# Seven products for five of the eight chunk pairs of a cosine layer, with the features kept in float32 until the last layer

## The chip, the cores and the metric

One core of one Trainium2 chip runs the program. The metric is the device time of one execution in microseconds (us), before and after the change.

## The reference

Causal attention (2 batches of 448 tokens, 12 heads of 64) is followed by a gated layer and by a layer with a cosine. What the change touches is the end:

```python
    gate = 1.0 / (1.0 + np.exp(-(x @ w_gate)))   # x: 896 x 768, w_gate and w_val: 768 x 1536
    val = x @ w_val
    x = gate * val @ w_out                        # w_out: 1536 x 768
    h = x @ w_in                                  # w_in: 768 x 2048
    g = h * np.cos(h)
    return g @ w_out2                             # 2048 x 768
```

(`w_in` and `w_out2` are the arrays `moe2_w_in` and `moe2_w_out`.) Inputs and output are of double and single precision; products must come out with nearly float32 accuracy.

## The kernel before, in words

Features lie on partitions, the 448 tokens of one batch on the free dimension. TensorE multiplies 128x128 blocks of weights (stationary) by 128x448 blocks of features (moving). To get nearly float32 accuracy, every float32 operand is split into a high and a low part: ScalarE rounds (`hi`), VectorE subtracts (`lo = x - hi`), and one product is three matmuls, hi·hi, hi·lo and lo·hi (`products`, lines 223 to 230). So one output block of 128 features for one batch in a layer with 768 inputs is 6 x 3 = 18 matmuls, a *group*.

The weights come from HBM in *chunks* (one block of outputs, up to six blocks of inputs) as raw 64-bit words. Each chunk is loaded by SyncE (line 144, two buffers `wraw`), decoded into float32 by ScalarE (upper half `up`, line 165) and VectorE (`wf`, line 167), and split into `whi` (ScalarE, line 176) and `wlo` (VectorE, line 178); four buffers each. `advance` (line 219) splits one chunk, decodes the next and loads the one after.

The order of the work is written out by hand. Each engine runs its own queue strictly in the order in which the program issues to it, and waits on semaphores. The stages:

- Attention, 0 to about 75 us.
- The gate layer (lines 544 to 647). Its first two of twelve outputs are plain, the other ten are *units* of class `Unit`: Strassen's algorithm on 2x2 blocks, where the two outputs are the gate and the value block, the two halves of the inputs are even and odd chunks (order `KORD`), and the two columns are the two batches. Seven products of 3 x 3 = 9 matmuls (`product`, line 491) replace eight. The price is sums of weights (`sums12`, `sums34`, 384 wide), three split weights per unit instead of two, and sums that are carried through PSUM banks: `after(n)` copies or adds a bank once product n is there, for instance line 537 adds bank `b` and the copy `s5` into a new bank `c`, and product 7 then goes on in bank `b`, product 3 in `c`. The products of a unit are issued in the order 1, 5, 2, 6, 4, 7, 3, where product 4 is the previous unit's; the first unit has no previous one and runs 1, 5, 6, 2, 7, 3. Between two products `emit` issues what follows the product before.
- The output layer (lines 655 to 670): 432 matmuls, two output blocks at a time, each split into `X2` at once.
- The cosine layer (lines 701 to 711): 16 outputs, two batches, plain groups. `post` follows each group on ScalarE and VectorE: `turns` (line 678 rounds h/2pi to an integer, line 679 subtracts it), `cosine` one group later (Sin at line 683, multiply by the bank at 684), and `split` of the feature g two groups later (lines 233 and 234).
- The last layer (lines 713 to 732): six outputs, one after the other, each over three chunks and two batches, then a copy and the output DMA.

Of the kernel before, what the change touches and what calls it, by code (L numbers as in the profile page):

```python
# [2 lines left out]

# [17 lines left out]
P = 128  # L21
# [14 lines left out]
KP = KX // 2  # L36
WH = KP * P
PLAIN = 2

FIRST_ROWS = {2: (0, 3), 4: (3, 5)}  # L40
FIRST_ROWS_END = 5
# [29 lines left out]
def attn_moe_moe2(  # L71
# [337 lines left out]
    early = ExitStack()  # L409
    epool = early.enter_context(tc.tile_pool(name="epool", bufs=1))  # L410
    epool.tile([P, 48], F32, tag="pad", name="pad")

    def temp(tag, bufs):
# [42 lines left out]
    class Unit:  # L456

        def __init__(self, f):
            self.f = f

        def parts(self, src):
            hi, lo = weights("whi"), weights("wlo")
# [35 lines left out]
                mm(ps[:, :S], lhsT=lo[:, blk], rhs=r[:, 0], start=False, stop=stop, skip_group_check=True)  # L498

        def p(self, n):  # L500
            x = [[XB[b][2 * j + o] for j in range(KP)] for o, b in ((0, 0), (1, 0), (1, 1))]
            if n == 1:
                self.a = bank()
                self.product(self.a, self.A, 0, x[0], True, True)
            elif n == 2:
                self.product(self.a, self.A, 1, x[1], False, True)
            elif n == 3:
                self.product(self.c, self.S34, 1, x[2], False, True)
            elif n == 4:
                self.product(self.e, self.A22, 0, T[3], False, True)  # L510
            elif n == 5:
                self.d = bank()
                self.product(self.d, self.S12, 0, T[0], True, True)
            elif n == 6:
                self.product(self.b, self.S12, 1, T[1], False, True)
            else:
                self.product(self.b, self.S34, 0, T[2], False, True)

        def after(self, n):
            if n == 1:  # L520
                self.b = bank()
                nc.scalar.copy(self.b[:, :S], self.a[:, :S])
            elif n == 2:
                self.sg0 = temp("sg", 4)
                nc.scalar.activation(self.sg0, self.a[:, :S], AF.Sigmoid)
            elif n == 3:
                sg1 = temp("sg", 4)
                nc.scalar.activation(sg1, self.c[:, :S], AF.Sigmoid)
                gated(self.f, 1, sg1, self.tmp)
            elif n == 4:  # L530
                gated(self.f, 0, self.sg0, self.e[:, :S])
            elif n == 5:
                self.s5 = temp("s5", 2)
                nc.scalar.copy(self.s5, self.d[:, :S])
            elif n == 6:
                self.c = bank()
                nc.vector.tensor_tensor(self.c[:, :S], self.b[:, :S], self.s5, op=ALU.add)
            else:
                self.e = bank()
                nc.scalar.copy(self.e[:, :S], self.b[:, :S])  # L540
                self.tmp = temp("tmp", 2)
                nc.vector.tensor_tensor(self.tmp, self.e[:, :S], self.s5, op=ALU.add)

    for f in range(PLAIN):
        sg = []
        if f:
            wt = next_chunk()
            pg = []
            advance()
        else:  # L550
            decode_load()
        for b in range(B):
            if f:
                pg.append(bank())
                products(pg[b], wt, xr[b], True, True)
            sg.append(temp("sg", 4))
            nc.scalar.activation(sg[b], pg[b][:, :S], AF.Sigmoid)
            run(3)
        wt = next_chunk()
        if f == PLAIN - 1:  # L560
            words = [singles[2 * PLAIN].w]
        advance()
        if f == PLAIN - 1:
            unit = Unit(PLAIN)
# [37 lines left out]
    def emit(u, n):  # L602
        u.p(n)
        if done:
            v, m = done.pop()
            v.after(m)
        done.append((u, n))

    old = None
    unit.A = next_chunk()  # L610
    for f in range(PLAIN, KH):
        new, last = Unit(f + 1), f == KH - 1
# [30 lines left out]
        unit, old = new, unit  # L643
    emit(old, 4)
    split_h(1)
    old.after(4)
    early.close()

    gpool = ctx.enter_context(tc.tile_pool(name="gpool", bufs=1))
    tpool = ctx.enter_context(tc.tile_pool(name="tpool", bufs=2))  # L650

    at_chunk["split"] = at_chunk["use"] = 2 * KH
    parts[step("split")] = new.A
    singles[2 * KH + 1] = k1
    X2 = [[None] * KX for b in range(B)]
    nch = KH // WC
    for m in range(0, KX, 2):
        ps2 = [[bank() for i in range(2)] for b in range(B)]
        for c in range(nch):
            wts = [next_chunk()]  # L660
            for b in range(B):
                advance()
                for i in range(2):
                    if i and not b:
                        wts.append(next_chunk())
                    products(ps2[b][i], wts[i], H[b][c * WC : c * WC + WC], c == 0, c == nch - 1)
                    split_h(3)
                    if c == nch - 1:
                        X2[b][m + i] = slot(f"f{2 * (m + i) + b}", f"y{m + i}{b}")
                        split(X2[b][m + i], ps2[b][i][:, :S])  # L670

    quarter = tpool.tile([P, 1], F32, tag="quarter", name="quarter", bufs=1)
    nc.vector.memset(quarter, TWOPI / 4)

    def turns(ph):
        r = tpool.tile([P, S], F32, tag="t1", name="r", bufs=3)
        n = r.bitcast(I32)
        nc.scalar.activation(n, ph[:, :S], AF.Copy, scale=INV2PI, bias=0.25)  # L678
        nc.vector.scalar_tensor_tensor(r, ph[:, :S], INV2PI, n, op0=ALU.mult, op1=ALU.subtract)  # L679
        return r  # L680

    def cosine(ph, r):
        nc.scalar.activation(r, r, AF.Sin, scale=TWOPI, bias=quarter)
        nc.vector.tensor_tensor(r, r, ph[:, :S], op=ALU.mult)

    GTAG = [f"g{i}" for i in range(8)] + list(HTAGS)
    G = [[None] * KG for b in range(B)]
    units = {}
    nu = KG * B

    def post(u):
        if u < nu:
            units[u].append(turns(units[u][0]))
        if 0 <= u - 1 < nu:
            cosine(*units[u - 1])
        if 0 <= u - 2 < nu:
            f, b = divmod(u - 2, B)
            G[b][f] = slot(GTAG.pop(0), f"g{f}{b}")
            split(G[b][f], units.pop(u - 2)[1])

    for f in range(KG):
        wt = next_chunk()
        for b in range(B):
            u = f * B + b
            units[u] = [bank()]
            products(units[u][0], wt, X2[b], True, True)
            if b == 0:
                advance()
            post(u)
    post(nu)  # L710
    post(nu + 1)

    nch = (KG + WC - 1) // WC
    for m in range(KX):
        ps2 = [bank(), bank()]
        for c in range(nch):
            wt = next_chunk()
            advance()
            for b in range(B):
                products(ps2[b], wt, G[b][c * WC : min(KG, c * WC + WC)], c == 0, c == nch - 1)  # L720
                if c == nch - 1:
                    o = tpool.tile([P, S], F32, tag="t0", name="o")
                    rows, c0 = slice(m * P, m * P + P), b * S
                    if m == KX - 1 and b == B - 1:

                        nc.scalar.copy(o[:, : S // 2], ps2[b][:, : S // 2])
                        nc.vector.tensor_copy(o[:, S // 2 :], ps2[b][:, S // 2 : S])
                        nc.scalar.dma_start(out=out[rows, c0 : c0 + S // 2], in_=o[:, : S // 2])
                        nc.sync.dma_start(out=out[rows, c0 + S // 2 : c0 + S], in_=o[:, S // 2 :])
                    else:  # L730
                        nc.scalar.copy(o, ps2[b][:, :S])
                        nc.sync.dma_start(out=out[rows, c0 : c0 + S], in_=o)

def _layouts(inputs):
# [19 lines left out]
    def blocks(w):  # L756
# [32 lines left out]
```

## Time and profile before

| | |
|---|---|
| median of 3 runs | 553.76 us (553.63 to 553.77) |
| profiled execution | 553.79 us, its span 551.9 us |
| TensorE busy (PE) | 545.4 us, 99%, 3104 matmuls |
| VectorE busy (DVE) | 334.0 us, 61% |
| ScalarE busy (ACT) | 301.7 us, 55% |
| GpSimd busy (POOL) | 59.2 us, 11% |
| DMA | 68.14 MB, mean 123 GB/s |

Busy time counts the time in which an engine works on an instruction. The span goes from the first to the last instruction that the profiler recorded; the execution's time holds some 1.9 us more around it. PEld is TensorE's weight load, which overlaps its matmuls. All times of rows count from the span's start.

### The profile page before, as it was taken

How to read it: one execution, taken by the hardware profiler on the slowest of the kernel's cores; microseconds unless marked ns; L12 is line 12 of the kernel's file. 1: busy time of each engine (PE TensorE's matmuls, PEld its weight loads, DVE VectorE, ACT ScalarE, POOL GpSimd, SP SyncE). 2: the span in 40 equal slices, each digit the busy share in tenths (PEclk: the TensorE clock that was granted, in tenths of full speed). 3: DMA queues.
4: the chain of work that ended last, by engine and by line, in shares of the span. 5: the costliest groups of instructions: out<-in, count | busy, mean ns of one | idle time of the engine just before them, and what ended most of it. 6: DMA issues, size and time to landing. Idle time of an engine off the chain costs nothing.

```text
span 551.9 us, 8126 instructions
## 1 busy us (share of the span) xinstructions
PE 545.4 (99%) x3104; PEld 489.1 (89%) x3104; DVE 334.0 (61%) x624; ACT 301.7 (55%) x579; POOL 59.2 (11%) x131
## 2 busy tenths in 40 slices
PE   8999999999999999999999999999999999999997
PEld 5666679989999999999999999999999999999996
DVE  4889959987777777873324257777777722312310
ACT  5898955675555665853323267666666632422320
POOL 4788850000000000000000000000000000000000
PEclk9999999999999999999999999999999999999999
DMA  8745114264433333351515123333333234532500
GB/s 337 261 147 211 50 58 130 99 184 142 132 115 115 114 116 115 115 172 57 173 57 172 47 69 116 113 115 114 116 114 97 83 113 143 186 116 87 169 34 33
DMA packets 14725, 68.14 MB, mean 123 GB/s; under 512 B 1632, under 2 KB 3808, under 8 KB 14688
## 3 DMA queue, kind: packets, MB, share of 16 engines
q1 hardware_dynamic: 14400, 67.33, 37.1%
q8 instruction: 24, 0.39, 0.3%
q10 hardware_dynamic: 288, 0.31, 0.2%
q14 instruction: 13, 0.11, 0.1%
HBM read 64.88 MB, written 2.75 MB: 123 GB/s over the span
## 4 chain that ended last, share of the span: by engine, by line
PE 97%; POOL 1%; ACT 1%; DVE 1%; issue 0%; ACTq 0%; POOLq 0%
PE ps L230 21%; PE ps L229 21%; PE ps L228 21%; PE ps L496 8%; PE ps L497 8%; PE ps L498 8%; PE ps L326 4%; PE ps L342 4%; PE ps L302 3%; POOL pbuf L286 1%; ACT pbuf L310 1%; PE ps L256 1%; DVE ps L306 0%; DVE rs L283 0%; POOL sums L282 0%
## 5 line engine op out<-in xcount | busy, mean ns | idle before, releaser
L178 DVE TENSOR_TENSOR wlo<-wf,whi 128x768 fp32r<-128x768 f32 (+2 forms) x51 | 47.3, 927 | 61.6 <-ACT whi L176 60.1
L165 ACT ACTIVATE up<-wraw 128x768 f16<-128x768 bf16 (+2 forms) x71 | 74.2, 1046 | 12.1 <-DMA wraw<-in_w_out_dram 10.7
L167 DVE SCALAR_TENSOR_TENSOR wf<-wraw,up 128x768 uint32<-128x768 uint32 (+2 forms) x71 | 66.9, 942 | 22.4 <-ACT up L165 21.8
L230 PE MATMUL ps<-g,wlo 128*128 128x448 f32 x192 | 69.7, 363 | 0.0
L230 PE MATMUL ps<-y,wlo 128*128 128x448 f32 x192 | 69.7, 363 | 0.0
L229 PE MATMUL ps<-y,whi 128*128 128x448 f32 x192 | 69.6, 362 | 0.0
L229 PE MATMUL ps<-g,whi 128*128 128x448 f32 x192 | 69.6, 362 | 0.0
L228 PE MATMUL ps<-y,whi 128*128 128x448 f32 x192 | 69.1, 360 | 0.0
L228 PE MATMUL ps<-g,whi 128*128 128x448 f32 x192 | 69.1, 360 | 0.0
L230 PE MATMUL ps<-h,wlo 128*128 128x448 f32 x144 | 52.3, 363 | 0.0
L229 PE MATMUL ps<-h,whi 128*128 128x448 f32 x144 | 52.2, 362 | 0.0
L228 PE MATMUL ps<-h,whi 128*128 128x448 f32 x144 | 51.8, 360 | 0.0
L176 ACT ACTIVATE whi<-wf 128x768 fp32r<-128x768 f32 (+2 forms) x51 | 41.0, 804 | 14.9 <-DVE wf L167 14.9
L310 ACT ACTIVATE pbuf<-ps,nm 128x64 f32<-128x64 f32 (+6 forms) x84 | 38.6, 482 | 9.6 <-DVE nm L306 9.1
L286 POOL TENSOR_SCALAR pbuf<-pbuf,rs 128x64 f32<-128x64 f32 (+6 forms) x84 | 39.1, 488 | 9.4 <-PE ps L302 6.3
L679 DVE SCALAR_TENSOR_TENSOR r<-ps,r 128x448 f32<-128x448 f32 x32 | 19.9, 621 | 31.3 <-ACT r L678 31.3
L678 ACT ACTIVATE r<-ps 128x448 int32<-128x448 f32 x32 | 17.4, 545 | 38.9 <-PE ps L230 38.9
L229 PEld LDWEIGHTS ps<-y,whi 128*128 128x128 f32 x192 | 36.0, 188 | 2.9
L229 PEld LDWEIGHTS ps<-g,whi 128*128 128x128 f32 x192 | 36.0, 188 | 2.9
L228 PEld LDWEIGHTS ps<-g,whi 128*128 128x128 f32 x192 | 35.9, 187 | 2.6
L228 PEld LDWEIGHTS ps<-y,whi 128*128 128x128 f32 x192 | 35.9, 187 | 2.4
L230 PEld LDWEIGHTS ps<-y,wlo 128*128 128x128 f32 x192 | 36.0, 188 | 2.0
(96 smaller groups left out, 1089.4 us busy)
## 6 DMA issues: line engine op xcount, KB each, us to landing
wraw<-in_w_gv_dram SPq DMA_DIRECT2D x24, 768.0 KB, 4.3
wraw<-in_w_out_dram SPq DMA_DIRECT2D x24, 768.0 KB, 4.4
wraw<-in_w_in_dram SPq DMA_DIRECT2D x16, 768.0 KB, 4.3
qkv<-in_qkv_dram SPq DMA_DIRECT2D x9, 928.0 KB, 5.9
wraw<-in_w_out_dram SPq DMA_DIRECT2D x6, 512.0 KB, 3.9
out_dram<-o SPq DMA_DIRECT2D x11, 224.0 KB, 2.0
qkv<-in_qkv_dram SPq DMA_DIRECT2D x3, 256.0 KB, 6.8
qkv<-in_qkv_dram SPq DMA_DIRECT2D x1, 672.0 KB, 6.4
```

The costliest lines, as they stand in the source:

```text
L165: nc.scalar.activation(up.bitcast(F16)[:, 1::2], self.top[:, e0:e1], AF.Copy)
L167: nc.vector.scalar_tensor_tensor(self.w[:, e0:e1].bitcast(U32), self.mid[:, e0:e1], 13, up.bitcast(U32), op0=ALU.logical_shift_right, op1= ...
L176: nc.scalar.activation(self.hi[:, e0:e1], self.w[:, e0:e1], AF.Copy)
L178: nc.vector.tensor_tensor(self.lo[:, e0:e1], self.w[:, e0:e1], self.hi.bitcast(F32)[:, e0:e1], op=ALU.subtract)
L228: mm(ps[:, :S], lhsT=hi[:, blk], rhs=r[:, 0], start=first and k == 0, stop=False)
L229: mm(ps[:, :S], lhsT=hi[:, blk], rhs=r[:, 1], start=False, stop=False)
L230: mm(ps[:, :S], lhsT=lo[:, blk], rhs=r[:, 0], start=False, stop=last and k == n - 1)
L286: nc.gpsimd.tensor_scalar(row, row, rs[:, i : i + 1], 1.0, op0=ALU.mult, op1=ALU.mult)
L310: nc.scalar.activation(pb[:, POFF[i] : POFF[i] + w], ps[:, :w], AF.Exp, scale=-1.0, bias=nm[:, i : i + 1], accum_out=sums[:, i : i + 1],)
L496: mm(ps[:, :S], lhsT=hi[:, blk], rhs=r[:, 0], start=start, stop=False, skip_group_check=True)
L497: mm(ps[:, :S], lhsT=hi[:, blk], rhs=r[:, 1], start=False, stop=False, skip_group_check=True)
L498: mm(ps[:, :S], lhsT=lo[:, blk], rhs=r[:, 0], start=False, stop=stop, skip_group_check=True)
```

## The change

`Unit` becomes a general class `Product` (features X and their sums T are its arguments), and the gate layer's units a subclass `Gate` that does the same as before. A second subclass `Pair` takes two output chunks of the cosine layer together. The string `KINDS` says for each of the eight pairs whether it goes by seven products (S: pairs 1, 2, 4, 5, 6, counted from 0) or plainly (P: pairs 0, 3, 7). The output layer makes also the sums of its results that the products need (`U2`, split into `T2`). The features g are no longer split when they are made but kept in float32 (`GF`), and split later (`split_g`): seven in the last pair, the rest in the last layer. That layer takes two outputs at a time, so each pair of chunks is used by four groups before the next. `w_in` comes in the order `KORD`.

```diff
+KINDS = "PSSPSSSP"
...
-    for m in range(KX):
+    for m in range(0, KX, 2):
         for c in range(0, KG, WC):
             n = min(WC, KG - c)
-            chunks.append((w_out2[m, :, c : c + n], n))
+            for i in range(2):
+                chunks.append((w_out2[m + i, :, c : c + n], n))
...
+    def block_of_x(j, ps, b, i):
+        X2[b][2 * j + i] = slot(XTAG[j][2 * b + i], f"y{2 * j + i}{b}")
+        split(X2[b][2 * j + i], ps[b][i][:, :S])
+        if not i:
+            if not b:
+                U2[j] = [slot(tag, "u", F32) for tag in UTAG[j]]
+            nc.scalar.copy(U2[j][0][:, b], ps[b][i][:, :S])
+            if b:
+                u1 = U2[j][0][:, 0]
+                difference(u1, ps[1][0][:, :S], u1)
+
+    def sums_of_block(j, ps):
+        (u1, u3), (u2, u4) = [[t[:, i] for i in range(2)] for t in U2[j]]
+        for dst, a, b in ((u3, ps[1][1], u3), (u2, ps[1][1], u1), (u4, ps[0][1], u2)):
+            difference(dst, a[:, :S], b)
+            yield
+
+    def parts_of_block(j):
+        (u1, u3), (u2, u4) = [[t[:, i] for i in range(2)] for t in U2[j]]
+        for i, u in enumerate((u1, u2, u3, u4)):
+            T2[i][j] = slot(TTAG[j][i], f"T{i}{j}")
+            split(T2[i][j], u)
+            yield
...
+    def cosines():
+        if turned:
+            h, r, (f, b) = turned.pop(0)
+            if GF[f] is None:
+                GF[f] = slot(GFTAG.pop(0), f"g{f}", F32)
+            nc.scalar.activation(r, r, AF.Sin, scale=TWOPI, bias=quarter)
+            nc.vector.tensor_tensor(GF[f][:, b], r, h, op=ALU.mult)
+        if due:
+            h, fb = due.pop(0)
+            r = temp("sg", 4)
+            n = r.bitcast(I32)
+            nc.scalar.activation(n, h, AF.Copy, scale=INV2PI, bias=0.25)
+            nc.vector.scalar_tensor_tensor(r, h, INV2PI, n, op0=ALU.mult, op1=ALU.subtract)
+            turned.append((h, r, fb))
...
+        def result(self, n):
+            f = self.f
+            if n == 2:
+                due.append((self.a[:, :S], (f, 0)))
+            elif n == 3:
+                due.extend([(self.c[:, :S], (f, 1)), (self.tmp, (f + 1, 1))])
+            elif n == 4:
+                due.append((self.e[:, :S], (f + 1, 0)))
...
+        if seven:
+            order = (1, 5, 2, 6, 4, 7, 3) if old else (1, 5, 6, 2, 7, 3)
+        else:
+            order = (8, 9, 4) + tuple(range(10, 16)) if old else tuple(range(8, 16))
+        for at, n in enumerate(order):
+            emit(old if n == 4 else unit, n)
+            cosines()
+            if at == 0:
+                if seven:
+                    unit.high22()
+                    k0 = upper_of()
+                    unit.sums34()
...
+            elif at == 1:
+                if seven:
+                    unit.S34 = unit.parts(unit.s34)
+                    unit.low22()
...
+                w0 = word_of(k0)
+            elif at == 2:
+                k1 = upper_of()
+                if seven:
+                    unit.low(unit.S34, unit.s34)
+            elif at == 3:
+                new.A = unit.parts(w0)
+                new.w = w0, word_of(k1)
+            elif at == 4 and new_seven:
+                new.sums12()
+            elif at == 5:
+                if new_seven:
+                    new.S12 = new.parts(new.s12)
+                unit.low(new.A, w0)
+            if at == min(len(order) - 1, 6) and new_seven:
+                new.low(new.S12, new.s12)
+            run(1)
+            if last and at > 1:
+                split_g(1)
...
+                for i in range(2):
+                    if i and not b:
+                        wts.append(next_chunk())
+                    g, m = G[b][c * WC : min(KG, c * WC + WC)], 2 * j + i
+                    products(ps2[b][i], wts[i], g, c == 0, c == nch - 1)
+                    cosines()
+                    split_g(3)
...
-        "w_in2": blocks(inputs["moe2_w_in"]),
+        "w_in2": blocks(inputs["moe2_w_in"])[:, :, list(KORD)],
```

Products 8 to 15 are the halves (9 matmuls) of a plain pair's four groups. After the change line 429 is `difference`, 171 and 182 are the decode and the low part in `Chunk`, 478 the first sum of `sums12`, 533 the sum for bank `c`, 538 that for `tmp`, 743 the subtraction of turns and 737 the multiply by the Sin.

First place: VectorE's queue in a plain pair of chunks of the cosine layer before. `wf` is a decoded chunk, `r` the turns and then the cosine, `g` a feature's split.

```order
L178 TENSOR_TENSOR wlo<-wf_3313,whi 128x768
L167 SCALAR_TENSOR_TENSOR wf_3375<-wraw,up 128x768
L679 SCALAR_TENSOR_TENSOR r<-ps,r 128x448
L684 TENSOR_TENSOR r<-r,ps 128x448
L234 TENSOR_TENSOR g_3384<-r,g_3384 128x448
```

And the second half of pair 4 in the changed kernel, which has six products (in the order 1, 5, 6, 2, 7, 3) because a plain pair stands before it:

```order
L533 TENSOR_TENSOR ps<-ps,s_3823 128x448
L171 SCALAR_TENSOR_TENSOR wf_3825<-wraw,up 128x768
L743 SCALAR_TENSOR_TENSOR sg<-ps,sg 128x448
L478 TENSOR_TENSOR s_3856<-wf_3825 128x384
L429 TENSOR_TENSOR s_3856<-s_3856,wf_3789 128x384
L538 TENSOR_TENSOR tmp<-ps,s_3823 128x448
L737 TENSOR_TENSOR g_3872<-sg,ps 128x448
L429 TENSOR_TENSOR wlo<-wf_3789,whi 128x768
L429 TENSOR_TENSOR wlo<-s_3856,whi 128x768
```

The split of the feature has gone, sums of weights and a second low part have come in, and a cosine's multiply (line 737) stands between the sum for `tmp` and the low part of the next pair's first weights.

Second place: VectorE's queue in pair 5 from the first subtraction of turns to the sum for bank `c` (line 533), on whose bank product 7 goes on.

```order
L743 SCALAR_TENSOR_TENSOR sg<-ps,sg 128x448
L429 TENSOR_TENSOR s_3897<-wf_3789,wf_3825 128x384
L429 TENSOR_TENSOR s_3897<-wf_3789,s_3856 128x384
L737 TENSOR_TENSOR g_3872<-sg,ps 128x448
L743 SCALAR_TENSOR_TENSOR sg<-tmp,sg 128x448
L429 TENSOR_TENSOR a_3893<-wf_3825,a_3893 128x384
L171 SCALAR_TENSOR_TENSOR wf_3895<-wraw,up 128x768
L737 TENSOR_TENSOR g_3934<-sg,tmp 128x448
L429 TENSOR_TENSOR wlo<-s_3897,whi 128x768
L743 SCALAR_TENSOR_TENSOR sg<-ps,sg 128x448
L171 SCALAR_TENSOR_TENSOR wf_3937<-wraw,up 128x768
L533 TENSOR_TENSOR ps<-ps,s_3932 128x448
```

In the gate layer the same stretch has one operation of 448 (the gated product) ahead of the two sums and none of the four others of lines 737 and 743 behind them.

## Rows read from the trace of the kernel before

**Rows 1.** The page: busy time of the engines, and the chain that ended last, by engine.

```profile
PE 545.4 (99%) x3104; PEld 489.1 (89%) x3104; DVE 334.0 (61%) x624; ACT 301.7 (55%) x579; POOL 59.2 (11%) x131
...
PE 97%; POOL 1%; ACT 1%; DVE 1%; issue 0%; ACTq 0%; POOLq 0%
```

**Rows 2.** Timeline of TensorE where the cosine layer begins: start, duration (us), line, operation.

```profile
317.60 0.36 PE L230 MATMUL ps<-h,wlo 128*128 128x448 f32 x1
317.80 0.36 PE L228 MATMUL ps<-y,whi 128*128 128x448 f32 x1
```

**Rows 3.** Windows (us; PE, PEld, DVE, ACT, POOL busy): output, cosine, last layer, gate unit.

```profile
231.30:317.80 86.50, 86.50 (x434) 81.08 (x433) 38.25 (x52) 33.38 (x50) 0.00 (x0) 1.00 0.35 110
317.80:433.00 115.20, 115.20 (x577) 107.98 (x576) 81.41 (x124) 76.28 (x124) 0.00 (x0) 1.00 0.32 105
433.00:548.20 115.20, 115.20 (x577) 107.79 (x575) 31.30 (x39) 36.13 (x50) 0.00 (x0) 1.00 0.34 110
...
153.80:166.40 12.60, 12.60 (x64) 11.81 (x63) 9.36 (x15) 7.30 (x11) 0.00 (x0) 1.00 0.39 125
```

**Rows 4.** Timeline of VectorE in a unit of the gate layer.

```profile
155.12 0.55 DVE L425 TENSOR_TENSOR s<-wf,wf 128x384 f32<-128x384 f32 x1
155.59 0.55 DVE L425 TENSOR_TENSOR s<-wf,s 128x384 f32<-128x384 f32 x1
...
156.53 0.95 DVE L167 SCALAR_TENSOR_TENSOR wf<-wraw,up 128x768 uint32<-128x768 uint32 x1
157.40 0.95 DVE L425 TENSOR_TENSOR wlo<-s,whi 128x768 fp32r<-128x768 f32 x1
...
161.74 0.55 DVE L474 TENSOR_TENSOR s<-wf 128x384 f32<-128x384 f32 x1
162.32 0.56 DVE L425 TENSOR_TENSOR s<-s,wf 128x384 f32<-128x384 f32 x1
```

**Rows 5.** Timeline of ScalarE and VectorE behind a group of the cosine layer.

```profile
350.40 0.55 ACT L678 ACTIVATE r<-ps 128x448 int32<-128x448 f32 x1 [0.32 <-PE ps L230]
...
350.84 0.66 ACT L683 ACTIVATE r<-r,quarter 128x448 f32<-128x448 f32 x1
...
350.99 0.62 DVE L679 SCALAR_TENSOR_TENSOR r<-ps,r 128x448 f32<-128x448 f32 x1
...
351.54 0.62 DVE L684 TENSOR_TENSOR r<-r,ps 128x448 f32<-128x448 f32 x1
```

**Rows 6.** Timeline of ScalarE in the unit of rows 4.

```profile
154.44 0.52 ACT L485 ACTIVATE a<-wf 128x384 fp32r<-128x384 f32 x1
154.86 1.08 ACT L165 ACTIVATE up<-wraw 128x768 f16<-128x768 bf16 x1
155.80 0.57 ACT L522 COPY ps<-ps 128x448 f32<-128x448 f32 x1
156.30 0.85 ACT L463 ACTIVATE whi<-s 128x768 fp32r<-128x768 f32 x1
```

**Rows 7.** Timelines of VectorE and TensorE at the end of the gate layer's first unit.

```profile
111.40 0.63 DVE L537 TENSOR_TENSOR ps<-ps,s 128x448 f32<-128x448 f32 x1
...
114.74 0.62 DVE L542 TENSOR_TENSOR tmp<-ps,s 128x448 f32<-128x448 f32 x1 [0.68 <-ACT ps L540]
115.29 0.95 DVE L425 TENSOR_TENSOR wlo<-wf,whi 128x768 fp32r<-128x768 f32 x1
...
112.08 0.47 PE L496 MATMUL ps<-T,whi 128*128 128x448 f32 x1
112.39 0.37 PE L497 MATMUL ps<-T,whi 128*128 128x448 f32 x1
...
116.29 0.47 PE L498 MATMUL ps<-x,wlo 128*128 128x448 f32 x1
116.60 0.36 PE L496 MATMUL ps<-x,whi 128*128 128x448 f32 x1
```

**Rows 8.** Groups of VectorE in the cosine layer: busy us, mean ns, idle before, releaser.

```profile
L679 DVE SCALAR_TENSOR_TENSOR r<-ps,r 128x448 f32<-128x448 f32 x31 | 19.3, 621 | 29.4 <-ACT r L678 29.4
```

More of the change, by code (lines that the diff above doesn't have):

```diff
@@ L509, in p, with behind @@
             elif n == 4:
-                self.product(self.e, self.A22, 0, T[3], False, True)
+                self.product(self.e, self.A22, 0, self.T[3], False, True)
             elif n == 5:
                 self.d = bank()
-                self.product(self.d, self.S12, 0, T[0], True, True)
+                self.product(self.d, self.S12, 0, self.T[0], True, True)
             elif n == 6:
-                self.product(self.b, self.S12, 1, T[1], False, True)
+                self.product(self.b, self.S12, 1, self.T[1], False, True)
             else:
-                self.product(self.b, self.S34, 0, T[2], False, True)
-        def after(self, n):
+                self.product(self.b, self.S34, 0, self.T[2], False, True)
+        def behind(self, n):
             if n == 1:
@@ L522, in after, with __init__ @@
                 nc.scalar.copy(self.b[:, :S], self.a[:, :S])
-            elif n == 2:
+            elif n == 5:
+                self.s5 = temp("s5", 2)
+                nc.scalar.copy(self.s5, self.d[:, :S])
+            elif n == 6:
+                self.c = bank()
+                nc.vector.tensor_tensor(self.c[:, :S], self.b[:, :S], self.s5, op=ALU.add)
+            elif n == 7:
+                self.e = bank()
+                nc.scalar.copy(self.e[:, :S], self.b[:, :S])
+                self.tmp = temp("tmp", 2)
+                nc.vector.tensor_tensor(self.tmp, self.e[:, :S], self.s5, op=ALU.add)
+            else:
+                self.result(n)
+    class Gate(Product):
+        def __init__(self, f):
+            Product.__init__(self, XB, T)
+            self.f = f
+        def result(self, n):
+            if n == 2:
                 self.sg0 = temp("sg", 4)
@@ L529, in after @@
                 gated(self.f, 1, sg1, self.tmp)
-            elif n == 4:
+            else:
                 gated(self.f, 0, self.sg0, self.e[:, :S])
[L532 to L542, printed above, removed]
     for f in range(PLAIN):
@@ L605, in emit @@
             v, m = done.pop()
-            v.after(m)
+            v.behind(m)
         done.append((u, n))
@@ L611, in attn_moe_moe2 @@
     for f in range(PLAIN, KH):
-        new, last = Unit(f + 1), f == KH - 1
+        new, last = Gate(f + 1), f == KH - 1
         order = (1, 5, 2, 6, 4, 7, 3) if old else (1, 5, 6, 2, 7, 3)
@@ L645, in attn_moe_moe2 @@
     split_h(1)
[L646 to L650, printed above, removed]
+    old.behind(4)
+    done.pop()
     at_chunk["split"] = at_chunk["use"] = 2 * KH
@@ L682, in cosine @@
[L682 to L686, printed above, removed]
-    G = [[None] * KG for b in range(B)]
[L688 to L707, printed above, removed]
-                advance()
[L709 to L732, printed above, removed]
@@ new lines, in attn_moe_moe2, with split_g @@
+    GTAG = ["b4", "f7", "b0", "b5", "f8", "b1", "t3", "f9", "b2", "t4", "t13", "t14"] + sum(XTAG, [])
+    GORD = [(k, b) for c in range(0, KG, WC) for b in range(B) for k in range(c, min(KG, c + WC))]
+    GFREE = ["t5", "t6", "t7", "t8", "b6", "b7", "b8", "t9", "t10", "t11", "g2", "g3", "f4", "f5"]
+    G = [[None] * KG for b in range(B)]
+    def split_g(n):
+        for i in range(n):
+            if GORD:
+                k, b = GORD.pop(0)
+                G[b][k] = slot(GTAG.pop(0), f"g{k}{b}")
+                split(G[b][k], GF[k][:, b])
+                if b == B - 1 and GFREE:
+                    GTAG.append(GFREE.pop(0))
@@ new lines, in attn_moe_moe2, with __init__, p, result @@
+    class Pair(Product):
+        def __init__(self, u):
+            Product.__init__(self, X2, T2)
+            self.f = 2 * u
+            self.xr = [[X2[b][k] for k in KORD] for b in range(B)]
+            self.banks = {}
+        def p(self, n):
+            if n <= 7:
+                return Product.p(self, n)
+            i, b, half = (n - 8) // 4, (n - 8) // 2 % 2, n % 2 == 1
+            if not half:
+                self.banks[i, b] = bank()
+            ks = range(half * KP, half * KP + KP)
+            products(self.banks[i, b], self.C if i else self.A, self.xr[b], not half, half, ks)
+        def result(self, n):
+            f = self.f
+            if n == 2:
+                due.append((self.a[:, :S], (f, 0)))
[3 more added lines that the diff above has]
+                due.append((self.e[:, :S], (f + 1, 0)))
+            elif n % 2:
+                i, b = (n - 8) // 4, (n - 8) // 2 % 2
+                due.append((self.banks[i, b][:, :S], (f + i, b)))
@@ new lines, in attn_moe_moe2 @@
+    c3 = at_chunk["use"]
+    unit, old = Pair(0), None
+    unit.A = next_chunk()
+    unit.w = None, singles.pop(c3 + 1).w
+    for u, kind in enumerate(KINDS):
+        new, last = Pair(u + 1), u == len(KINDS) - 1
+        seven = kind == "S"
+        new_seven = not last and KINDS[u + 1] == "S"
+        if seven:
+            order = (1, 5, 2, 6, 4, 7, 3) if old else (1, 5, 6, 2, 7, 3)
+        else:
+            order = (8, 9, 4) + tuple(range(10, 16)) if old else tuple(range(8, 16))
[7 more added lines that the diff above has]
+                    unit.sums34()
+                else:
+                    unit.C = unit.parts(unit.w[1])
+                    k0 = upper_of()
+            elif at == 1:
+                if seven:
+                    unit.S34 = unit.parts(unit.s34)
+                    unit.low22()
+                else:
+                    unit.low(unit.C, unit.w[1])
+                w0 = word_of(k0)
[14 more added lines that the diff above has]
+                new.low(new.S12, new.s12)
+            run(1)
+            if last and at > 1:
+                split_g(1)
+        unit, old = new, unit if seven else None
@@ new lines, in attn_moe_moe2 @@
+    c4 = c3 + KG
+    at_chunk["split"] = at_chunk["use"] = c4
+    parts[step("split")] = unit.A
+    singles[c4 + 1] = k1
+    v, n = done.pop()
+    v.behind(n)
+    nch = (KG + WC - 1) // WC
+    for j in range(KP):
+        ps2 = [[bank() for i in range(2)] for b in range(B)]
+        for c in range(nch):
+            wts = [next_chunk()]
+            for b in range(B):
+                advance()
+                for i in range(2):
[5 more added lines that the diff above has]
+                    split_g(3)
+                    if c == nch - 1:
+                        o, ps = temp("sg", 4), ps2[b][i]
+                        rows, c0 = slice(m * P, m * P + P), b * S
+                        if m == KX - 1 and b == B - 1:
+                            nc.scalar.copy(o[:, : S // 2], ps[:, : S // 2])
+                            nc.vector.tensor_copy(o[:, S // 2 :], ps[:, S // 2 : S])
+                            nc.scalar.dma_start(out=out[rows, c0 : c0 + S // 2], in_=o[:, : S // 2])
+                            nc.sync.dma_start(out=out[rows, c0 + S // 2 : c0 + S], in_=o[:, S // 2 :])
+                        else:
+                            nc.scalar.copy(o, ps[:, :S])
+                            nc.sync.dma_start(out=out[rows, c0 : c0 + S], in_=o)
```

42 lines of the change are left out of this document (25 added, 17 removed).

## The prediction, made before the changed kernel ran

> **What bounds the kernel now.** I read the page first: TensorE is busy 99% of the span and carries 97% of the chain that ended last [rows 1], so only fewer matmuls, or a TensorE that waits, can move the time. The timeline of TensorE across the start of the cosine layer gives the price of one matmul: starts are 0.200 us apart, also over the border of two layers [rows 2]. (The 0.36 us of a row is its modelled duration, matmuls overlap.) The windows by layer check it: the cosine layer has 576 matmuls of 448 columns in 115.2 us, the last layer as many in 115.2 us, the clock at its full 2.4 GHz throughout (1.00) [rows 3]. VectorE and ScalarE have much room in both, 81.4 and 76.3 us busy of 115.2, then 31.3 and 36.1.
>
> The gate layer does already what the cosine layer is to do. A unit of seven products takes 12.6 us there and busies VectorE for 9.4 us of it [rows 3]. To price a queue I need the distance of starts, not durations: in the gate unit a 384-wide VectorE operation lasts 0.55 us, but the next starts 0.47 us after it, and a 768-wide one 0.95 and 0.87 [rows 4]; a 448-wide one lasts 0.62 and is followed after 0.55 [rows 5]. ScalarE: 0.42 us behind the 384-wide copy, 0.94 behind the 768-wide decode, 0.50 behind a 448-wide copy [rows 6]; 0.44 behind the rounding, whose consumer on VectorE starts 0.04 us after its end [rows 5]. A bank is picked up 0.20 us after the next product begins (317.80 plus nine groups of 3.6 us is 350.20; ScalarE starts at 350.40) [rows 2, 5].
>
> **The change part by part.**
>
> *Matmuls.* The pairs count from 0; 1, 2, 4, 5 and 6 get seven products. A plain pair is 2 x 2 x 6 x 3 = 72 matmuls, a pair by seven products 7 x 3 x 3 = 63. Five pairs save 45; the order of the changed kernel has just 45 fewer. 45 x 0.200 = **-9.0 us**, all on the path.
>
> *Output layer.* Per block pair it adds two ScalarE copies, four differences and four splits; over three block pairs (the last one's sums run into the first pair of the cosine layer) 18 ScalarE operations at 0.57 us and 24 VectorE ones at 0.62, some 10 and 15 us, in a layer where VectorE is busy 38.3 us of 86.5 [rows 3]. Nothing on TensorE follows from them before the second pair: I take 0. Without that cover it would be a few tenths.
>
> *Last layer.* 25 of the 32 splits of features move here: 25 x 0.62 = 15.5 us on VectorE beside 31.3, 25 x 0.57 = 14.2 on ScalarE beside 36.1, of 115.2 [rows 3]. They stand three to a group of 18 matmuls (3.6 us), before the group that reads them. 0, if the seven splits in the last pair come in time (a rival below). The chunks' order leaves loads, output DMAs and the end as they were: 0.
>
> *VectorE in a seven-product pair.* Two decodes and three low parts at 0.87, two pairs of 384-wide sums and one low part (0.47 each, 0.58 where one needs the other), two 448-wide sums and, new, eight operations for four cosines at 0.55: about 12.25 us in 12.6. It fits with 0.35 us to spare, so what counts is when each result is due. I walk the queue, in us from the pair's first matmul; two results come late.
>
> *Late result 1, a six-product pair (pairs 1 and 4).* The low part of the next pair's first weights is due at that pair's third matmul. The gate's first unit has the same order and just misses: the sum from the copied bank starts at 114.74, the low part at 115.29, it ends 116.24, and the matmul starts at 116.29, not 116.20; the one behind it 0.31 us later, not 0.20 [rows 7]. It loses 0.2 in all. The change puts one multiply of 0.55 between the two (order, first place). Loss 0.75, twice: **+1.5 us**.
>
> *Late result 2, pairs 2, 5 and 6.* The product behind A22's writes on the bank that the sum for `c` reads, and is due after five products, at 9.0. ScalarE reaches the bank of the first product at 2.0, copies, and starts the first Sin at 2.5, done 3.16. VectorE (first subtraction of turns and two sums behind it) waits for that Sin until 3.20, idle for about half a us. Then, one after the other: multiply, subtraction, low part 384, decode at 4.75 (ends 5.70), multiply 5.62, low part of S34 6.16. The second chunk's upper half can only be written when the decode has read the first: ScalarE 5.74 to 6.82, rounding 6.68 to 7.23; subtraction 7.27, second decode 7.82, the sum 8.69, done 9.32. A product has followed such a sum by 0.05 us in the gate's first unit (111.40 + 0.63, start 112.08), and its second matmul came 0.1 us late [rows 7]: start 9.37, loss 0.47, three times: **+1.4 us**. The low parts after it have about 1 us in hand, so the loss does not grow from pair to pair.
>
> Bounds for these five: not under 0.1 each, what the gate's miss cost at its mildest, 0.5 together; above, 4.9 (next part). I take the walk, 2.9.
>
> *Sum.* -9.0 + 1.5 + 1.4 = -6.1. The profiled execution took 553.79 us (span 551.9); 547.7. The median of the three runs is 553.76, the same within 0.03, so **547.7**.
>
> **The rivals.**
>
> *VectorE operations do not overlap beside waits.* If each holds the queue for its whole duration, a full pair costs VectorE 13.8 us, not 12.25. Late result 1 grows by two overlaps of 0.08 to 0.9; in late result 2 the chain from 3.20 runs 3.82, 4.45, 5.00, the decode ends 5.96, the second upper half 7.08, the rounding 7.63, the sum 9.88: loss 1.03. Together 1.8 + 3.1 = 4.9: 549.7. For it: many of the new operations wait for a Sin or a rounding first. Against: 0.47 behind 0.55 in a layer of the same build [rows 4]. Chance 0.15. The Trainium skill, "VectorE: DVE Perf Modes", section "The DRAIN you can't avoid", says that after an operation the next does not start until the pipe is empty; the trace's starts inside the duration before them speak against reading that as whole durations, and by it one would come to this rival.
>
> *The misses stay as small as in the gate layer*, 0.1 each, because ScalarE's Sin comes earlier than I placed it: 545.3. Chance 0.12.
>
> *The last layer starts late.* Its first group needs the first sixth of the features split; the sixth split stands behind the rounding of a bank that is ready 3.6 us before the layer. By the rows the chain of rounding, subtraction and split (0.55, 0.62, 0.57, 0.62) ends about 1 us early. If VectorE carries a lag there, TensorE waits once, by some 1.4 us (0.2 + 0.57 + 0.62): 549.1. Chance 0.07.
>
> *Slower: the cosines' hand-overs hold VectorE.* Today VectorE stands before the subtraction of turns for 29.4 us over 31 of them, 0.95 each [rows 8], harmless with the room it has. If each of a pair's four did so in the full queue, the pair would need 12.25 + 3.8 = 16.05 us against 12.6, 3.45 too many, 17 us over five: 562. From (12.6 + 1.8 - 12.25) / 4 = 0.54 us each the pair loses its nine matmuls. Against: there VectorE has nothing to do until its bank is ready; in the new order decodes and sums stand ahead (order, second place), and the walk finds 0.5 us of waiting once and 0.25 once in a pair. Chance 0.05.
>
> That fewer matmuls are not issued is excluded by the order.
>
> **How the numbers follow.** Forecast 0.61 at 547.7 (own range 546.3 to 549.2), overlapping operations gone 0.15 at 549.7, small misses 0.12 at 545.3, late last layer 0.07 at 549.1, slower 0.05. From 545.0 to 550.3 all but the slower case and the upper end of the first rival is taken in. Faster or slower counts over 0.2%, 1.1 us, about what a measurement here can tell: every case but the last is faster, by 4 us or more; a mild form of it gives no change. Faster 0.93, same 0.03, slower 0.04.
>
> **What would show it.** A cosine layer of 531 matmuls in about 109 us (106.2 and the 2.9 of waits); TensorE's waits there on the low part of the next pair's weights (pairs 1 and 4) and on the sum for `c` (2, 5, 6), each under 1 us; VectorE over 90% busy in pairs 4 to 6; output and last layer at 86.4 and 115.2 us. Wrong would be: a wait over 1.8 us in each seven-product pair, waits in plain pairs, or a last layer that starts on a wait for a feature.

## The result, and the profile after

The changed kernel takes 547.72 us (547.67 to 547.74, 4 runs) against 553.76 us: a ratio of 0.9891, 95% interval 0.9874 to 0.9908. The forecast was 547.7 us. The profiled span fell from 551.9 to 545.9 us.

The windows of the changed kernel, cut at the first matmul of each layer (output, cosine, last layer; the last window is the run of pairs 4 to 6; columns as in rows 3):

```profile
231.34:317.74 86.40, 86.40 (x434) 81.03 (x432) 47.34 (x69) 40.02 (x63) 0.00 (x0) 1.00 0.35 110
317.74:427.08 109.34, 107.50 (x532) 99.22 (x531) 92.56 (x149) 81.39 (x132) 0.00 (x0) 1.00 0.35 116
427.08:542.28 115.20, 115.20 (x577) 107.81 (x575) 42.98 (x62) 45.13 (x72) 0.00 (x0) 1.00 0.32 105
373.00:410.88 37.88, 36.78 (x181) 33.54 (x181) 33.17 (x54) 28.36 (x46) 0.00 (x0) 1.00 0.39 126
```

Against [rows 3] only the cosine layer has changed its length: 109.34 us instead of 115.20. Of its 531 matmuls at 0.200 us, 106.2 us, the rest, 3.14 us, is waiting. The output layer is as long as before although VectorE does 9 us more in it, and the last layer too, with 12 us more. The granted clock was 1.00 in all four windows, the 2.4 GHz level.

The waits of TensorE in the changed kernel, in its list of waits, name two operations of VectorE in the cosine layer:

```profile
PE ps L502 <- DVE wlo L429: 1.0, 2, 0.5
PE ps L500 <- DVE ps L533: 0.8, 3, 0.3
```

Twice on a low part of weights, three times on the sum for bank `c`. The list counts only the time in which the modelled matmul before had ended. The whole loss is read from the distance of starts in the timeline, less 0.200. The first place of each kind, pair 1 into pair 2, and pair 2 (VectorE's rows first, then TensorE's):

```profile
341.89 0.62 DVE L538 TENSOR_TENSOR tmp<-ps,s 128x448 f32<-128x448 f32 x1
342.48 0.62 DVE L737 TENSOR_TENSOR g<-sg,ps 128x448 f32<-128x448 f32 x1
343.01 0.95 DVE L429 TENSOR_TENSOR wlo<-wf,whi 128x768 fp32r<-128x768 f32 x1
...
342.94 0.36 PE L500 MATMUL ps<-y,whi 128*128 128x448 f32 x1
343.14 0.37 PE L501 MATMUL ps<-y,whi 128*128 128x448 f32 x1
344.02 0.47 PE L502 MATMUL ps<-y,wlo 128*128 128x448 f32 x1 [0.51 <-DVE wlo L429]
344.33 0.37 PE L500 MATMUL ps<-y,whi 128*128 128x448 f32 x1
...
349.82 0.95 DVE L429 TENSOR_TENSOR wlo<-s,whi 128x768 fp32r<-128x768 f32 x1
350.95 0.62 DVE L743 SCALAR_TENSOR_TENSOR sg<-ps,sg 128x448 f32<-128x448 f32 x1 [0.18 <-ACT sg L742]
351.49 0.95 DVE L171 SCALAR_TENSOR_TENSOR wf<-wraw,up 128x768 uint32<-128x768 uint32 x1
352.36 0.63 DVE L533 TENSOR_TENSOR ps<-ps,s 128x448 f32<-128x448 f32 x1
352.89 0.61 DVE L737 TENSOR_TENSOR g<-sg,ps 128x448 f32<-128x448 f32 x1
...
352.54 0.37 PE L502 MATMUL ps<-T,a 128*128 128x448 f32 x1
353.13 0.44 PE L500 MATMUL ps<-T,whi 128*128 128x448 f32 x1 [0.23 <-DVE ps L533]
353.41 0.36 PE L501 MATMUL ps<-T,whi 128*128 128x448 f32 x1
```

The low part ends at 343.96, the matmul that reads it starts at 344.02 instead of 343.34, the next one 0.31 us later: 0.68 + 0.11 = 0.79 us lost. It is [rows 7] over again with the multiply of line 737 in between. The sum ends at 352.99, the product on its bank starts at 353.13 instead of 352.74: 0.39 + 0.08 = 0.47. Over all five places, from the same kind of rows:

| place | forecast | measured |
|---|---|---|
| low part, pair 1 into 2 | 0.75 | 0.79 |
| low part, pair 4 into 5 | 0.75 | 0.79 |
| sum for c, pair 2 | 0.47 | 0.47 |
| sum for c, pair 5 | 0.47 | 0.48 |
| sum for c, pair 6 | 0.47 | 0.60 |
| together | 2.9 | 3.13 |

Pair 6 is the one place that is off by more than 0.05 us, and the only one of the three sums whose pair begins on time. Its first matmul, its sum, and the product behind the sum:

```profile
397.68 0.36 PE L500 MATMUL ps<-y,whi 128*128 128x448 f32 x1
...
406.43 0.63 DVE L533 TENSOR_TENSOR ps<-ps,s 128x448 f32<-128x448 f32 x1
...
407.20 0.45 PE L500 MATMUL ps<-T,whi 128*128 128x448 f32 x1 [0.35 <-DVE ps L533]
```

From the output layer's first matmul to the end no other start is more than 0.025 us late. Ahead of it, the gate layer's last product loses 0.2 us, before as after.

### The profile page after: what moved, and what is told of

The parts are those of the page before. It is cut to its first block, busy times and chain, and to the rows that moved or that the text cites. A ratio compares the mean times of both kernels' runs of the same rounds, so it can differ in the third digit from the quotient of the medians.

```text
span 545.9 us, 8155 instructions
## 1 busy us (share of the span) xinstructions
PE 537.0 (98%) x3059; PEld 480.0 (88%) x3059; DVE 366.0 (67%) x688; ACT 322.5 (59%) x622; POOL 59.2 (11%) x131
## 4 chain that ended last, share of the span: by engine, by line
PE 91%; DVE 3%; ACT 3%; issue 1%; POOL 1%; DVEq 0%; ACTq 0%; POOLq 0%
PE ps L234 17%; PE ps L233 17%; PE ps L232 17%; PE ps L500 10%; PE ps L502 10%; PE ps L501 10%; PE ps L330 4%; PE ps L346 4%; PE ps L306 3%; POOL pbuf L290 1%; DVE wf L171 1%; ACT up L169 1%; ACT pbuf L314 1%; PE ps L260 1%; DVE sg L743 0%
## 5 line engine op out<-in xcount | busy, mean ns | idle before, releaser
L171 DVE SCALAR_TENSOR_TENSOR wf<-wraw,up 128x768 uint32<-128x768 uint32 (+2 forms) x71 | 66.7, 940 | 13.9 <-ACT up L169 13.7
L182 DVE TENSOR_TENSOR wlo<-wf,whi 128x768 fp32r<-128x768 f32 (+2 forms) x35 | 31.9, 912 | 46.6 <-ACT whi L180 45.9
L500 PE MATMUL ps<-T,whi 128*128 128x448 f32 x135 | 49.3, 365 | 0.8 <-DVE ps L533 0.8
L501 PE MATMUL ps<-T,whi 128*128 128x448 f32 x135 | 49.0, 363 | 0.0
L502 PE MATMUL ps<-T,wlo 128*128 128x448 f32 x135 | 48.7, 361 | 0.0
L467 ACT ACTIVATE whi<-s 128x768 fp32r<-128x768 f32 x30 | 25.3, 842 | 24.7 <-DVE s L429 24.6
L871 ACT COPY sg<-ps 128x448 f32<-128x448 f32 x11 | 5.9, 534 | 54.0 <-PE ps L234 53.7
L234 PEld LDWEIGHTS ps<-g,wlo 128*128 128x128 f32 x192 | 36.0, 188 | 2.0
L180 ACT ACTIVATE whi<-wf 128x768 fp32r<-128x768 f32 (+2 forms) x35 | 27.6, 788 | 14.5 <-DVE wf L171 7.8
L310 DVE CUSTOM_DVE_ANT_0 ps<-ps,mask 128x64 f32<-128x64 f32 (+6 forms) x84 | 32.7, 457 | 2.9 <-PE ps L306 2.8
L501 PE MATMUL ps<-x,whi 128*128 128x448 f32 x90 | 32.7, 363 | 0.0
```

Source lines behind the costliest of these rows:

```text
L171: nc.vector.scalar_tensor_tensor(self.w[:, e0:e1].bitcast(U32), self.mid[:, e0:e1], 13, up.bitcast(U32), op0=ALU.logical_shift_right, op1= ...
L182: nc.vector.tensor_tensor(self.lo[:, e0:e1], self.w[:, e0:e1], self.hi.bitcast(F32)[:, e0:e1], op=ALU.subtract)
L310: nc.vector.tensor_tensor_reduce(out=ps[:, :w], in0=ps[:, :w], in1=mask[:, S - w :], scale=-0.125, scalar=3.0e38, op0=ALU.add, op1=ALU.min ...
L500: mm(ps[:, :S], lhsT=hi[:, blk], rhs=r[:, 0], start=start, stop=False, skip_group_check=True)
L501: mm(ps[:, :S], lhsT=hi[:, blk], rhs=r[:, 1], start=False, stop=False, skip_group_check=True)
```

## The experiments

A forecast can be right by luck. The theory says that the gain is matmuls alone, and that the five losses come from the *places* of two operations in VectorE's queue. The rival says that VectorE's *throughput* is exhausted, so that only less work on it would help. The times of each kernel are medians beside runs of the kernel before on the same chip (553.65 us for the first four, 553.73 for the next three, 553.72 for the last). The changed kernel's 547.72 stands beside 553.76, so a difference to it is uncertain by about 0.1 us.

### All pairs plain: is the gain matmuls alone?

```diff
-KINDS = "PSSPSSSP"
+KINDS = "PPPPPPPP"
```

> All eight pairs plain, so 576 matmuls in the cosine layer as before; the float32 features, their late split, the output layer's extra sums (still made, read by nobody) and the last layer by chunk pairs stay. My theory (those parts cost nothing, the gain is matmuls alone): 553.7 us, within 0.3 of the kernel before, and no gap between matmul starts over 0.225 us from the output layer to the end. Rival (the new order of the last layer or the early pool saves or costs something by itself): more than 0.5 us off 553.76, and so as much less or more of the 6.0 us is due to the matmuls.

Measured: 554.02 us, ratio 1.0007 (0.9998 to 1.0015): 0.37 us over the kernel before on the same chip, where 0.3 was expected at most, and not to be told from none. The cosine layer takes 115.2 us again (317.92 to 433.12), with less of VectorE and ScalarE in it than [rows 3] (a window as long as the layer, from three matmuls ahead of it):

```profile
317.30:432.50 115.20, 115.20 (x577) 107.98 (x577) 71.33 (x108) 68.08 (x105) 0.00 (x0) 1.00 0.34 111
```

No start is late from the output layer's first matmul on. So the float32 features, their late split, the output layer's sums and the new order of the last layer make TensorE wait nowhere and gain nothing by themselves here (0.37 us lost by the medians, 0.8 at most by the interval); the 6 us come from the seven products.

### Six pairs: does the loss grow along a run?

```diff
-KINDS = "PSSPSSSP"
+KINDS = "PSSSSSSP"
```

> Pair 3 goes by seven products too: one run of six. The total loses 9 more matmuls (1.8 us), pair 4 becomes a full unit instead of a six-product one. My theory (single results come late by their place in VectorE's queue, and the loss of a full pair does not grow): late result 1 once, 0.8; the sum for bank c five times, 0.5 to 0.6 each; 546.5 us. Rival (VectorE's throughput is exhausted, the lag builds up along a run of full pairs): each pair of the run loses more than the one before, over 1 us from the third on, and the time is 548 or more, no better than now.

Measured: 546.81 us, ratio 0.9877 (0.9862 to 0.9892). The low part costs 0.79 once; the sum for `c` costs 0.48, 0.60, 0.60, 0.88 and 0.60 in pairs 2 to 6. It does not build up, which is what the theory expected, but 0.3 us stay over: pair 5 of this run is worse by 0.28 than its neighbours. There ScalarE takes up a finished bank 0.54 us after the next product's first matmul (383.34), not 0.2:

```profile
383.88 0.55 ACT L742 ACTIVATE sg<-ps 128x448 int32<-128x448 f32 x1 [0.87 <-PE ps L502]
```

What held it is not settled. Nine matmuls fewer, 1.8 us, and 0.9 us gained.

### The low part earlier, in pairs of six products

```diff
                 new.w = w0, word_of(k1)
+                if seven and not old:
+                    unit.low(new.A, w0)
...
-                unit.low(new.A, w0)
+                if old or not seven:
+                    unit.low(new.A, w0)
```

> In the six-product pairs (1 and 4) the low part of the next pair's first weights is issued right behind the second decode, ahead of a cosine, two sums and a sum for tmp. VectorE has the same work. My theory (it was late by its place): the two gaps of 0.8 us in TensorE's starts vanish, the three on bank c stay at about 0.5, 546.2 us. Rival (throughput): VectorE finishes the rest as much later, the loss moves to the next pair's S12 or to bank c, and the time stays within 0.4 us of 547.7.

Measured: 546.10 us, ratio 0.9864 (0.9851 to 0.9878). Both gaps of 0.79 are gone; the sum for `c` costs 0.53, 0.53 and 0.61. VectorE's rows show the low part 3.5 us earlier than in the changed kernel, where it stood idle for 0.56 us (338.61 + 0.95 to 340.12):

```profile
338.62 0.95 DVE L171 SCALAR_TENSOR_TENSOR wf<-wraw,up 128x768 uint32<-128x768 uint32 x1
339.49 0.95 DVE L429 TENSOR_TENSOR wlo<-wf,whi 128x768 fp32r<-128x768 f32 x1
340.35 0.62 DVE L743 SCALAR_TENSOR_TENSOR sg<-ps,sg 128x448 f32<-128x448 f32 x1
```

The same work in another order brings 1.6 us. The rival falls for these pairs. Pairs 2 and 5 now begin on time as well, and their sums cost 0.53, not the 0.47 and 0.48 of the changed kernel.

### The sum for bank c ahead of the second decode, in full pairs

```diff
                 new.A = unit.parts(w0)
-                new.w = w0, word_of(k1)
-            elif at == 4 and new_seven:
-                new.sums12()
+                if not (seven and old):
+                    new.w = w0, word_of(k1)
+            elif at == 4:
+                if seven and old:
+                    new.w = w0, word_of(k1)
+                if new_seven:
+                    new.sums12()
```

> In full seven-product pairs (2, 5, 6) the second decode is issued behind the sum for bank c instead of ahead of it. VectorE has the same work; the sum ends 0.87 us earlier. My theory: the three gaps on bank c (0.47, 0.48, 0.60) vanish, the two on the low part stay at 0.8, 546.2 us. Rival (throughput): the sums of weights that need that decode come as much later, TensorE waits for the low part of S12 or of the next first weights instead, and the time stays within 0.4 us of 547.7.

Measured: 546.05 us, ratio 0.9864 (0.9851 to 0.9878). In pair 5 the sum now starts 1.2 us before its product, which starts on time:

```profile
392.00 0.62 DVE L533 TENSOR_TENSOR ps<-ps,s 128x448 f32<-128x448 f32 x1
...
393.03 0.36 PE L502 MATMUL ps<-T,a 128*128 128x448 f32 x1
393.23 0.36 PE L500 MATMUL ps<-T,whi 128*128 128x448 f32 x1
```

The three losses of 0.47 to 0.60 are gone (one start is 0.05 late), the two of 0.79 stay, as expected.

### Both orders

The two edits above together.

> The two reorderings together: the low part of the next first weights behind the second decode in six-product pairs, and the second decode behind the sum for bank c in full pairs. VectorE's work and the matmuls are those of the changed kernel. My theory (five results late by their place, 3.1 us in all): no gap over 0.25 us left in the cosine layer, 544.5 us. Rival (one of the two gained only because the other still gave VectorE time to catch up): the two gains of 1.6 and 1.7 us do not add, and a gap of 0.4 us or more comes back in pairs 2, 5 or 6; 545.2 or more.

Measured: 544.72 us, ratio 0.9837 (0.9824 to 0.9851). Against the kernel before on each chip the two edits alone brought 7.55 and 7.60 us, the changed kernel 6.04 and both together 9.01: gains of 1.5 and 1.6 add to 3.0, within 0.1. Against the expectation of no gap over 0.25, one start of the cosine layer is late, by 0.1 us (397.61), in pair 6:

```profile
397.30 0.47 PE L502 MATMUL ps<-T,wlo 128*128 128x448 f32 x1
397.61 0.36 PE L500 MATMUL ps<-T,whi 128*128 128x448 f32 x1
```

### Both orders and six pairs

The edits above and the string of the second experiment.

> Both reorderings and pair 3 by seven products too, a run of six. My theory: 9 matmuls less than with both alone, 1.8 us, and as VectorE needs 12.25 of a full pair's 12.6 us, no loss that grows: 542.7 us. Rival (VectorE's throughput): without the waits of TensorE that gave it time, VectorE falls behind along the run; gaps appear in pairs 4 to 6 and grow, up to the 0.35 us or more that its spare time would have to be overestimated by; 543.7 or more.

Measured: 543.96 us, ratio 0.9824 (0.9811 to 0.9838), 1.3 us over the theory's time and within the rival's. Pair 3 loses 0.11 us, pairs 4, 5 and 6 lose 0.31, 0.31 and 0.32, in small delays such as this one (a third matmul that waits for the low part of S12):

```profile
396.24 0.37 PE L501 MATMUL ps<-T,whi 128*128 128x448 f32 x1
396.57 0.47 PE L502 MATMUL ps<-T,wlo 128*128 128x448 f32 x1
396.88 0.37 PE L500 MATMUL ps<-T,whi 128*128 128x448 f32 x1
```

From pair 4 on the loss does not grow, it is a pace: pairs are 12.92 to 12.94 us apart, and so is VectorE's queue, in which the trace marks only two waits, both for ScalarE:

```profile
383.49 0.62 DVE L743 SCALAR_TENSOR_TENSOR sg<-ps,sg 128x448 f32<-128x448 f32 x1
...
387.90 0.96 DVE L429 TENSOR_TENSOR wlo<-s,whi 128x768 fp32r<-128x768 f32 x1
389.04 0.62 DVE L743 SCALAR_TENSOR_TENSOR sg<-ps,sg 128x448 f32<-128x448 f32 x1 [0.18 <-ACT sg L742]
389.58 0.62 DVE L533 TENSOR_TENSOR ps<-ps,s 128x448 f32<-128x448 f32 x1
390.40 0.62 DVE L737 TENSOR_TENSOR g<-sg,ps 128x448 f32<-128x448 f32 x1 [0.20 <-ACT sg L736]
...
396.43 0.62 DVE L743 SCALAR_TENSOR_TENSOR sg<-ps,sg 128x448 f32<-128x448 f32 x1
```

From 383.49 to 396.43 are 12.94 us. A wait costs more than the idle time in its brackets, since the overlap with the operation before is lost too: the first start comes 1.14 us after the one before it (387.90 to 389.04) where it comes after 0.87 without a wait (387.05 to 387.92 in the last experiment), the second 0.82 us after (389.58 to 390.40) where it came after 0.53 in the changed kernel (352.36 to 352.89). That is 0.27 and 0.29 us for the waits, and the operations alone come to about 12.4 us, not the 12.25 of the forecast.

Part of the difference stands in the distances that the forecast took for granted: 0.98 behind a decode whose result the next operation reads (not 0.87), 0.60 behind the sum for `tmp` (not 0.55). So VectorE's queue does set the pace here, as the rival has it, but with its two waits for ScalarE in it; its work alone would fit into the 12.6 us of a pair's matmuls.

### The gate layer's first unit as well

In the gate layer's loop: `if not old: unit.low(new.A, w0)` behind the second decode, and `if old:` before the old place.

> As the six pairs with both reorderings, and in the gate layer's first unit too the low part of the next unit's first weights is issued right behind the second decode. My theory: the gap of 0.2 us in all that stood in the rows of the kernel before at 116.29 vanishes, 542.5 us. Rival (the work that VectorE has there, splits of the sums T, only moves the wait): no change beside the six pairs with both reorderings.

Measured: 543.75 us, ratio 0.9818 (0.9805 to 0.9832), on the same chip as the two before. The expected 542.5 us were out of reach with the 1.3 us of the run before still there. The gap of [rows 7] at 116.29 is gone from the starts, and nothing has taken its place; 0.2 us is what the time moved too. A difference this small is carried by the rows more than by the times.

### The rounding of the turns ahead of the second upper half

```diff
             elif at == 2:
-                k1 = upper_of()
+                if not (seven and old):
+                    k1 = upper_of()
...
             elif at == 3:
+                if seven and old:
+                    k1 = upper_of()
                 new.A = unit.parts(w0)
```

> As the run before (six pairs, both reorderings, the gate layer's low part early), but in full pairs the upper half of the second chunk is issued on ScalarE behind the rounding of the turns of product 2 instead of ahead of it, where it waited for VectorE's first decode. VectorE's work is the same. In the run before a full pair took 12.93 us at a VectorE that waited only 0.18 us for that rounding and 0.20 us for the Sin behind it. My theory (VectorE sets the pace of the run, its operations alone need 12.55 us, under the 12.6 of the matmuls): both waits go, the four losses of 0.33 us vanish, 542.5 us. Rival (VectorE's operations alone need over 12.6 us, or the upper half now comes late for the second decode): the period stays over 12.8 us and the time over 543.3.

Measured: 542.60 us, ratio 0.9800 (0.9786 to 0.9813). The losses of 0.31 are gone; one start is 0.03 late. VectorE's queue in a full pair of this kernel, behind the sum for `c` of the pair before:

```profile
375.79 0.62 DVE L533 TENSOR_TENSOR ps<-ps,s 128x448 f32<-128x448 f32 x1
...
387.05 0.95 DVE L429 TENSOR_TENSOR wlo<-s,whi 128x768 fp32r<-128x768 f32 x1
387.92 0.62 DVE L746 SCALAR_TENSOR_TENSOR sg<-ps,sg 128x448 f32<-128x448 f32 x1
388.45 0.62 DVE L533 TENSOR_TENSOR ps<-ps,s 128x448 f32<-128x448 f32 x1
389.27 0.62 DVE L740 TENSOR_TENSOR g<-sg,ps 128x448 f32<-128x448 f32 x1 [0.20 <-ACT sg L739]
```

The wait of 0.18 for the rounding is gone, the one of 0.20 for the Sin stayed; against the expectation one wait was enough. The expectation had the operations alone at 12.55 us; with one wait left, losses would then have remained. From sum to sum (375.79 to 388.45) the queue now takes 12.66 us, 0.28 of it for the Sin, so again about 12.4 for the work. That is 0.06 more than a pair's matmuls: VectorE falls behind by so little that in a run of five full pairs one start shows it, in the last of them. Three full pairs (37.80 us) keep it busy for 37.00 (a window of the run):

```profile
357.90:395.70 37.80, 37.80 (x190) 35.27 (x189) 37.00 (x61) 30.67 (x52) 0.00 (x0) 1.00 0.38 126
```

This version beats both kernels: 11.1 us under the kernel before, 5.1 us under the changed one.

## Why the prediction was right, point by point

- **The bound.** Right. TensorE carried 97% of the chain [rows 1], and the time moved by matmuls saved and waits added: 45 x 0.200 less 3.13 is 5.87, and the cosine layer became 5.86 us shorter. The other 0.18 of the 6.04 us lie outside the layer and were not forecast, and the five waits were 0.23 us more than the 2.9 of the sum. These two misses nearly cancel: that the total came out within 0.02 us is luck.
- **Matmuls, -9.0 us.** Right: 531 instead of 576, and the all-plain kernel shows that the other parts of the change bring none of it.
- **Output and last layer, 0.** Right. Both layers kept their length, 86.4 and 115.2 us. VectorE's additions were smaller than forecast, 9 us instead of 15 and 12 instead of 15.5. The rival of a late last layer did not come: its first matmul (427.08) follows the one before (426.88) by 0.20 us.
- **Late result 1, +1.5 us.** Right in place and size, 1.58; that the place decides is shown by the kernel that moves it (546.10).
- **Late result 2, +1.4 us.** Right in place, 1.55 measured. That the place decides is shown by the kernel that moves it (546.05). The walk itself was good: the sum started 8.75 us after pair 6's first matmul (406.43 less 397.68), where it said 8.69. Too small was the hand-over to the product, 0.05 us in the forecast and 0.14 to 0.15 in all three pairs (406.43 + 0.63 to 407.20): hence 0.60 in pair 6. In pairs 2 and 5 the match to 0.01 us is luck. They begin with the 0.79 of late result 1, which the walk did not follow into them; less those 0.79, the sum of pair 2 started 8.63 us after the first matmul (352.36 less 342.94), and this made up for the hand-over. With the low part mended they lose 0.53.
- **12.25 us of VectorE in a full pair.** Mis-sized by about 0.15: 12.4 us alone, and 12.9 with the two waits for ScalarE, which this sum left out. "0.35 us to spare" was 0.2, and less than the waits need. In the changed kernel it did not matter: with TensorE's own wait a full pair took 13.2 us or more, and "the loss does not grow from pair to pair" held. Without that wait, in the run of six with both orders, pairs 4 to 6 lost 0.31 us each.
- **VectorE over 90% busy in pairs 4 to 6.** It was 33.17 of 37.88 us, 88%.
- **The rival of operations that do not overlap** forecast 549.7 us. (By the durations its full pair is 13.7 us, not 13.8.) It falls by its own rows: the decode starts 0.54 us after an operation of 0.62 (350.95 to 351.49) that had waited for ScalarE, and the sum 0.87 after the decode of 0.95. The Trainium skill's page "VectorE: DVE Perf Modes", section "The DRAIN you can't avoid", from which the prediction took that the next operation waits for an empty pipe, adds that a next operation that is not held starts earlier. This trace agrees, by these starts.
- **The small misses** (545.3 us) did not come: each loss was within 0.13 us of the size that the walk gave.
- **The slower rival**, cosines that hold VectorE: over the whole layer it waits 4.0 us for roundings (9 waits) and 9.4 us for Sins (11 waits; list of waits), but most of that in the plain and six-product pairs. A full pair has one wait of each, as the walk had it: 0.57 (346.87) and 0.18 (350.95) in pair 2, 0.60 and 0.18 in pair 6. That is 0.2 us for each of four cosines, far from the 0.54 at which a pair would lose its gain.

## What to carry to other kernels

When an engine's queue is nearly full, price a change by the distance of starts in a stretch of the same build, then walk the queue for the few results that another engine is waiting for: the walk gave each of five waits to 0.13 us or better, while the sum of the work, off by only 0.15 us, gave none of them. A wait that stands just behind an operation nobody is waiting for yet is mended by exchanging the two, at no cost in work; here that was worth half of the change's own gain. Only then is it time to ask whether the engine's throughput is the limit. A loss that is the same in each repetition does not show it: the run of six lost 0.31 us in each pair while its queue waited for ScalarE, and a third exchange ended that. Compare the time that the queue's operations take without their waits, 12.4 us here, with the time that there is, 12.6.

## What the runs showed of the hardware that was not expected

A TensorE that is late for its weights loses more than the delay: in the changed kernel the matmul behind the late one started 0.31 us after it instead of 0.20 (344.02 to 344.33 and 384.89 to 385.20). Where the bank was late it was 0.28 in the cosine layer (353.13 to 353.41) and 0.31 in the gate layer's first unit (112.08 to 112.39 in [rows 7]). What makes the difference is not known. And an operation of VectorE that reads what the one before it wrote did not start inside that one's duration in these traces: it came 0.98 us behind the 0.95 us decode (390.94 to 391.92 in the run of six with both orders), where others follow after 0.87, and 0.59 behind a sum of 0.56 (391.92 to 392.51), where others follow after 0.47.
